# Second MLP of a three-block layer chain: other operand sums, relu placement, loads and residual adds on other engines

## The chip, the cores and the metric

The kernel runs on one core of one Trainium2 chip. The metric is the device time of one execution in microseconds; the figure of the kernel before is the median of three runs. A core has TensorE (PE, matmuls), VectorE (DVE), ScalarE (ACT), GpSimd (POOL) and SyncE (SP, which here only issues DMAs). The first four run their own instruction streams, each in order, and wait for each other by semaphores.

## The reference, cut to what matters

Three blocks follow each other on 8 sequences of 576 tokens and 512 channels: a linear attention, a gated MLP, and the block that the change is about:

```python
xt = x.transpose(0, 2, 1)
h = xt @ U @ V                          # token mixing of rank 32
u = x + h.transpose(0, 2, 1)
ch = np.maximum(u @ w_ch1, 0.0) @ w_ch2 # 512 -> 2048 -> 512
return (u + ch).astype(np.float32)
```

## The kernel before

All work up to `u` (attention, gated MLP, token mixing) takes the first 650 us; `u` is then in DRAM (`u2d`), transposed, channels on partitions, split into two token halves. What follows is `relu(u @ w_ch1) @ w_ch2`, in **5 groups** of columns: four of 480 and one of 384 tokens out of each half (`GROUPS`, L41).

**Seven products in place of eight.** Each of the two matrix products is done on 2 x 2 blocks with seven block products (indices 1 to 7, in the order 1, 2, 6, 7, 5, 4, 3, L42) by Winograd's form of Strassen's scheme. The operands of the products are sums and differences of the blocks of `u` (first product) or of relu'd `h` (second product): h11, h12, h21, h22. The weights' sums are made once, during the last sequences and the first group ("the conversion", `more`, L970: pieces that load, convert on VectorE, ScalarE and GpSimd, and store to the DRAM tiles `wd`).

**High and low operands.** For accuracy each fp32 operand is split into a high part of reduced precision (a ScalarE copy, `oh` or `uh`) and a low part, the rest (one VectorE operation, `ol` or `ul`); a product is high x high + low weight x high + high weight x low. So each step needs one ScalarE copy and then one VectorE "low" for its operand.

**Steps.** A group has 56 steps of 12 matmuls: 28 of the first product (for each of j = 0..3, a quarter of the middle layer, the seven indices), then 28 of the second (for each index, the four j). Below, r is the number of a step in its group, 0 to 55. In a step, `products` (L869) issues the matmuls and `after` (L935) what follows them. In the first product `after` drains PSUM on VectorE: partial sums `kept` and blocks `h`. In the second product the four j of an index accumulate in one PSUM buffer (four buffers exist), drained at j = 3; the finished block is added to the residual `u` (`store_res`, L916) and stored.

**Order.** In the loop over steps (L1256 on) VectorE, ScalarE, GpSimd and SyncE run in the order in which the program is written (`in_order`, L1003). In step s come: the weight fetch for step s + 4 on SyncE (`fetch`, five buffers `RING`; it waits for the matmuls of step s - 1), pieces of the conversion while there are any (two per step), the operand for step s + 3 (`h_prep`, L829; four buffers `OPS`), one of the sums in `later` (`h_diff`, L858), the matmuls, and `after`.

**Where things are made.** relu is taken again in each use: by ScalarE in the copy (L839), by VectorE in an operation that takes max(., 0) and adds or subtracts (`relu_minus`, L816); only h12 is relu'd in place by ScalarE (L946). For index 6, `h_prep` makes a temporary t and updates h21 besides the low (L848 to L856). The next group's blocks of `u` are loaded on GpSimd's queue (`u_load`, L745) and split and summed in half-width pieces during the second product (`u_prep`, L766; 22 VectorE operations). The residual is loaded on GpSimd's queue (L914), the kept sums are added to it by GpSimd (`with_kept`, L932), and GpSimd's queue stores the result (L926).

Of the kernel before, what the change touches and what calls it, by code (L numbers as in the profile page):

```python
# [22 lines left out]
def fused_kernel(tc, q, k, v, w_in, g_ln, w_sgT, b_sg, w_out, U, V, w_ch1, w_ch2, outT):  # L23
# [792 lines left out]
    def relu_minus(out, a, b, op=ALU.subtract):  # L816
        dve.scalar_tensor_tensor(out=out, in0=a, scalar=0.0, in1=b, op0=ALU.max, op1=op)  # L817

# [7 lines left out]
    def h_tile(j, slot, n):  # L826
        return ht[j, slot][:, :, 0:n]

    def h_prep(s):  # L829

        g, _, j, a = steps[s]
        n = GROUPS[g]
        hi, lo = (p2["ops"].tile([P, 2, NM], F32R, tag=x, name=x, bufs=OPS) for x in ("oh", "ol"))
        hs[s] = (hi, lo)
        hi, lo = hi[:, :, 0:n], lo[:, :, 0:n]
        h11, h12, h21, h22 = (h_tile(j, x, n) for x in (11, 12, 21, 22))
        if a in (1, 2, 3):
# [4 lines left out]
        if a == 5:  # L842
            act.activation(hi, h11, AF.Copy, scale=-1.0)
            dve.scalar_tensor_tensor(
                out=lo, in0=h11, scalar=-1.0, in1=as_f32(hi), op0=ALU.mult, op1=ALU.subtract
            )
            return
        if a == 6:  # L848
            t = p2["ops"].tile([P, 2, NM], F32, tag="t2", name="t2", bufs=1)[:, :, 0:n]
            relu_minus(t, h22, h11, ALU.add)  # L850
        else:
            t = {7: h12, 4: h21}[a]
        copy(hi, t)
        if a == 6:
            relu_minus(h21, h21, t)
        low(dve, lo, t, hi)  # L856

    def h_diff(g, j):  # L858

        n = GROUPS[g]  # L860
        h11, h12, h22 = (h_tile(j, x, n) for x in (11, 12, 22))
        relu_minus(h11, h11, h12)
        yield
        relu_minus(h12, h22, h12)
        yield
# [42 lines left out]

    def load_res(g, slot):
        n = GROUPS[g]  # L910
        mh, th = HALF[slot]
        t0 = starts[g]
        r = res[slot] = p2["res"].tile([P, 2, NM], F32, tag="res", name="res", bufs=2)[:, :, 0:n]
        pool.dma_start(r, u2d[th, 2 * mh : 2 * mh + 2, :, t0 : t0 + n].rearrange("c p t -> p c t"))  # L914

    def store_res(g, slot, bank):  # L916
        n = GROUPS[g]
        mh, th = HALF[slot]
        r = res.pop(slot)
        tt(dve, r, bank, r, ALU.add)  # L920
        t = starts[g]
        while t < starts[g] + n:
            b = t // HS
            e = min((b + 1) * HS, starts[g] + n)
            o = b * S + th * HS + t - b * HS
            pool.dma_start(  # L926
                outT[2 * mh : 2 * mh + 2, :, o : o + e - t].rearrange("c p t -> p c t"),
                r[:, :, t - starts[g] : e - starts[g]],
            )
            t = e  # L930

    def with_kept(slot, k):  # L932
        tt(pool, res[slot], res[slot], kept[k], ALU.add)

    def after(s):  # L935

        g, i, j, a = steps[s]
        n = GROUPS[g]
        bank = ps[a][:, :, 0:n]
        if i == 0:  # L940
            if a in PART:
                slot, k = PART[a]
                h = h_out(j, slot, n)
                tt(dve, h, bank, kept[k], ALU.add)
                if a == 3:
                    act.activation(h, h, AF.Relu)  # L946
            partial(a, n)
            return
        if j == 0 and a in (1, 2, 5, 4):
            load_res(g, {1: 11, 2: 22, 5: 21, 4: 12}[a])  # L950
        if j < NJ - 1:
            return
        if a in PART:
            store_res(g, PART[a][0], bank)
        partial(a, n)
        if a == 1:
            with_kept(11, 1)
        elif a == 7:
            with_kept(22, 7)
        elif a == 5:  # L960
            with_kept(21, 7)
        elif a == 4:
            with_kept(12, 1)
# [46 lines left out]
    OPS = 4  # L1010
# [237 lines left out]
    pool2("ust", 2, side="right")  # L1248
# [5 lines left out]
    later = deque()  # L1254
    ust_load = u_load(p2["ust"], 2)
    for s in range(len(ORDER), len(steps)):  # L1256
# [3 lines left out]
        if pieces or loaded or bounded or begun or merged or stores:  # L1260
            more(2)
# [5 lines left out]
        if ahead_s < len(steps) and steps[ahead_s][1] == 1 and r + OPS - 1 >= half_steps:  # L1267
            if r + OPS - 1 == half_steps:
                later.clear()
# [3 lines left out]
            if later:  # L1273
                if next(later[0], 0) == 0:
                    later.popleft()
                    if later:
                        next(later[0])
        products(s)
        after(s)
        if i == 1 and g + 1 < len(GROUPS):  # L1280
            if a == 7:
                if j == 0:
                    prep = u_prep(g + 1, (ust_load, ust_load))
                    next(prep)
            elif a in (5, 4, 3):
                for _ in range(2):
                    next(prep, None)
            if r == PER - 1:
                run(prep)
# [43 lines left out]
```

## Time and profile before

| | |
|---|---|
| median of the runs | 1401.33 us (1400.21 to 1406.36, 3 runs) |
| the profiled execution | 1399.94 us |
| its span, first to last instruction | 1398.1 us |
| mean granted TensorE clock | 0.986 of full speed; full from 650 us on |
| busy: PE, DVE, ACT, POOL | 1298.7, 1049.2, 605.0, 487.9 us |
| DMA traffic | 269 MB, mean 193 GB/s |

Busy times are sums over the whole span; the stages differ. A "window" row gives, for a stretch from A to B us, its length and then for each engine the busy time in it and the number of instructions that touch it. In lists of groups a row gives engine, operation, output<-inputs, shape, count, then busy us and mean ns of one, then the idle time before them and what ended it. In timelines a row gives start, duration, engine, line.

### The profile page before, as it was taken

What the parts mean: (1) busy time and instruction counts of PE and PEld (TensorE: products, weight loads), DVE (VectorE), ACT (ScalarE), POOL (GpSimd) and SP (SyncE); (2) the same over time, 40 slices, a digit from 0 to 9 for tenths busy, and PEclk for the clock granted to TensorE, in tenths of its full rate; (3) what the DMA queues carried; (4) which work ended last, traced back from release to release, by engine and by line L of the source; (5) the groups of instructions that cost most, each with busy time, mean ns of one, the idle gap of its engine ahead of it and who ended that gap; (6) DMA issues with size and microseconds to landing.
All of it is one profiled execution on the core that took longest, in us unless ns stands there. A gap on an engine that the chain in (4) does not pass through costs nothing.

```text
span 1398.1 us, 20610 instructions
## 1 busy us (share of the span) xinstructions
PE 1298.7 (93%) x7576; PEld 1150.5 (82%) x7576; DVE 1049.2 (75%) x1481; ACT 605.0 (43%) x969; POOL 487.9 (35%) x522
## 2 busy tenths in 40 slices
PE   4679999999999999967999999999999999999998
PEld 3578988889898988866887888878887888789987
DVE  7878868686868787686889864888469954986584
ACT  3764747474757565644333421243123411242132
POOL 5954455445444545574331210123003300131013
PEclk9889999999999999988999999999999999999999
DMA  7514243343433332348996876677667766688776
GB/s 241 166 33 145 61 153 112 103 132 102 125 109 111 121 107 99 135 159 278 343 361 224 294 241 205 211 260 257 210 202 256 255 229 204 201 277 283 248 241 206
DMA packets 116691, 269.16 MB, mean 193 GB/s; under 512 B 11888, under 2 KB 39824, under 8 KB 116592
## 3 DMA queue, kind: packets, MB, share of 16 engines
q1 hardware_dynamic: 109392, 240.53, 52.2%
q0 software_dynamic: 7200, 27.33, 5.8%
q8 instruction: 60, 0.98, 0.3%
q14 instruction: 39, 0.32, 0.1%
HBM read 219.58 MB, written 48.23 MB: 192 GB/s over the span
## 4 chain that ended last, share of the span: by engine, by line
PE 54%; DVE 23%; ACT 7%; issue 7%; POOL 5%; DMA 5%; SPq 0%; ACTq 0%; DVEq 0%; POOLq 0%
PE mm L49 37%; PE pv L49 6%; PE py L49 4%; DVE h L817 3%; DVE ol L52 2%; DVE ol L817 2%; PE px L49 2%; POOL qt L52 2%; DMA stg<-in_w_ch_dram 1%; DVE t L817 1%; DVE f L179 1%; DVE qt L52 1%; PE pp L49 1%; DVE gl L52 1%; DVE ul L52 1%
## 5 line engine op out<-in xcount | busy, mean ns | idle before, releaser
L49 PE MATMUL mm<-oh,wu 128*128 128x480 f32 (+1 forms) x1120 | 325.2, 371 | 5.4 <-ACT oh L58 5.4
L49 PE MATMUL mm<-uh,wu 128*128 128x480 f32 (+1 forms) x1064 | 308.4, 371 | 0.7 <-DVE h L52 0.7
L49 PEld LDWEIGHTS mm<-oh,wu 128*128 128x128 f32 x1120 | 207.4, 188 | 35.6 <-ACT oh L58 11.6
L49 PE MATMUL mm<-ol,wu 128*128 128x480 f32 (+1 forms) x560 | 211.0, 377 | 11.3 <-DVE ol L52 9.8
L49 PEld LDWEIGHTS mm<-uh,wu 128*128 128x128 f32 x1064 | 198.1, 188 | 27.2 <-DVE h L52 1.0
L49 PE MATMUL mm<-ul,wu 128*128 128x480 f32 (+1 forms) x532 | 198.1, 372 | 0.0
L52 POOL TENSOR_TENSOR res<-res,u 128x960 f32<-128x960 f32 (+1 forms) x20 | 58.6, 2928 | 377.0 <-ACT u L58 312.1
L52 DVE TENSOR_TENSOR h<-mm,u 128x960 f32<-128x960 f32 (+1 forms) x76 | 84.6, 1113 | 89.5 <-PE mm L49 89.4
L946 ACT ACTIVATE h<-h 128x960 f32<-128x960 f32 (+1 forms) x20 | 19.5, 974 | 265.2 <-DVE h L52 265.2
L49 PEld LDWEIGHTS mm<-ol,wu 128*128 128x128 f32 x560 | 105.0, 188 | 34.6 <-DVE ol L52 18.9
L52 POOL TENSOR_TENSOR chw<-f,chw 128x256 fp32r<-128x256 f32 x112 | 88.7, 807 | 99.2 <-ACT chw L58 93.5
L52 DVE TENSOR_TENSOR u<-mm,u 128x960 f32<-128x960 f32 (+1 forms) x72 | 80.0, 1111 | 48.7 <-PE mm L49 48.6
L49 PEld LDWEIGHTS mm<-ul,wu 128*128 128x128 f32 x532 | 99.9, 188 | 12.3
L926 POOL DMA_DIRECT2D out_dram<-res x44 | 31.9, 727 | 160.2 <-DVE res L52 160.2
L817 DVE SCALAR_TENSOR_TENSOR ol<-h,oh 128x960 fp32r<-128x960 f32 (+1 forms) x60 | 72.4, 1208 | 11.4 <-ACT oh L839 11.2
L58 ACT ACTIVATE chw<-f 128x256 fp32r<-128x256 f32 x112 | 43.3, 411 | 76.7 <-DVE f L180 23.4
L49 PE MATMUL py<-gh,wo_h 128*128 128x288 f32 x256 | 59.0, 313 | 14.4 <-ACT gh L58 5.2
L785 ACT ACTIVATE uh<-ust 128x480 fp32r<-128x480 f32 (+1 forms) x63 | 34.2, 578 | 70.4 <-DVE ust L52 70.4
L52 DVE TENSOR_TENSOR ul<-ust,uh 128x480 fp32r<-128x480 f32 (+1 forms) x54 | 58.3, 1111 | 7.8 <-ACT uh L785 7.8
L49 PE MATMUL py<-gl,wo_h 128*128 128x288 f32 x256 | 56.4, 303 | 8.3 <-DVE gl L52 8.1
L49 PE MATMUL pS<-sg_h,vh 128*128 128x288 f32 x256 | 55.8, 300 | 4.7 <-ACT ut L628 4.7
L52 POOL TENSOR_TENSOR vl<-ge,vh 128x512 fp32r<-128x512 f32 x32 | 46.0, 1439 | 35.8 <-ACT vh L58 35.7
(176 smaller groups left out, 2991.4 us busy)
## 6 DMA issues: line engine op xcount, KB each, us to landing
wu<-wd SPq DMA_DIRECT2D x280, 512.0 KB, 3.9
wd<-chw SPq DMA_DIRECT2D x112, 256.0 KB, 2.6
stg<-in_w_ch_dram SPq DMA_DIRECT2D x64, 256.0 KB, 3.0
u2d<-yt SPq DMA_DIRECT2D x32, 288.0 KB, 2.3
vt<-in_v_dram SPq DMA_DIRECT2D x32, 256.0 KB, 6.5
res<-u2d POOLq DMA_DIRECT2D x16, 480.0 KB, 5.0
qt<-in_q_dram SPq DMA_DIRECT2D x7, 1024.0 KB, 6.3
kt<-in_k_dram SPq DMA_DIRECT2D x7, 1024.0 KB, 6.1
```

Source lines behind the costliest of these rows:

```text
L49: pe.matmul(out, lhsT, rhs, start=first, stop=last)
L52: return eng.tensor_tensor(out=out, in0=a, in1=b, op=op)
L58: return act.activation(out, src, AF.Copy)
L179: dve.tensor_scalar(out=b, in0=b, scalar1=3, scalar2=None, op0=ALU.logical_shift_left)
L785: act.activation(hi, t, AF.Copy, scale=-1.0 if neg else 1.0)
L817: dve.scalar_tensor_tensor(out=out, in0=a, scalar=0.0, in1=b, op0=ALU.max, op1=op)
L926: pool.dma_start(outT[2 * mh : 2 * mh + 2, :, o : o + e - t].rearrange("c p t -> p c t"), r[:, :, t - starts[g] : e - starts[g]],)
L946: act.activation(h, h, AF.Relu)
```

## The change

The same products in the same order, with these differences:

- **Sums of h from other pairs, in place** (`h_sum`, `H_SUMS`): 7: h12 = h22 - h12; 6: h11 = h12 + h11; 4: h21 = h21 - h11; 5: h11 = h22 - h11. They stand at steps of their own: three sums 7 in the first product (r = 8, 15, 22), the rest at r = 28 + the key of `H_SUMS`. No temporary t.
- **relu on ScalarE, in place, for all four blocks** (`due`, `relu_due`), so a copy and a low are plain.
- **`OPS` five** instead of four: the operand for step s + 4 is prepared in step s.
- **The next group's `u`** in one tile of full width: loaded at r = 7 on SyncE's queue, summed in place by GpSimd at r = 12, 14, 16, 18 of the first product, copied and lowered at fixed steps of the second; three blocks are loaded again after their sums were used (for indices 1, 2, 3).
- **Residual**: loads and stores on SyncE's queue, stores issued one step later (`sent`, `send`); kept sums added by VectorE (`RES_KEPT`); slot 11 takes the index-1 product straight from PSUM. The last store of the kernel is made in two halves.
- **Conversion**: two pieces a step, three at every fourth step.

```diff
-        h11, h12, h21, h22 = (h_tile(j, x, n) for x in (11, 12, 21, 22))
-        if a in (1, 2, 3):
-            t = {1: h11, 2: h21, 3: h22}[a]
-            act.activation(hi, t, AF.Relu)
-            relu_minus(lo, t, as_f32(hi))
-            return
...
+        t = h_tile(j, {1: 11, 2: 21, 6: 11, 7: 12, 5: 11, 4: 21, 3: 22}[a], n)
+        copy(hi, t)
+        low(dve, lo, t, hi)
+
+    def h_sum(a, j, n):
+
+        h11, h12, h21, h22 = (h_tile(j, x, n) for x in (11, 12, 21, 22))
+        if a == 7:
+            tt(dve, h12, h22, h12, ALU.subtract)
+        elif a == 6:
+            tt(dve, h11, h12, h11, ALU.add)
+        elif a == 4:
+            tt(dve, h21, h21, h11, ALU.subtract)
+        else:
+            tt(dve, h11, h22, h11, ALU.subtract)
+
+    H_SUMS = {
+        -2: (6, 0), -1: (6, 1), 0: (6, 2), 1: (7, 3), 2: (6, 3), 4: (4, 0), 5: (4, 1), 6: (5, 0), 8: (4, 2),
+        9: (4, 3), 10: (5, 1), 12: (5, 2), 13: (5, 3),
+    }
...
+    U_AT = {6: (0, 0), 4: (1, 0), 5: (1, 1), 7: (0, 1), 1: (0, 0), 2: (1, 0), 3: (1, 1)}
+    U_LOW = {14: 6, 17: 4, 18: 5, 20: 7, 22: 1, 24: 2, 25: 3}
+    U_HIGH = {x - 2: a for x, a in U_LOW.items()}
+    U_SUMS = {12: 7, 14: 6, 16: 4, 18: 5}
...
+    def u_fetch(g, h, j):
+        n, t0 = GROUPS[g], starts[g]
+        sp.dma_start(u_at(h, j, n), u2d[j, 2 * h : 2 * h + 2, :, t0 : t0 + n].rearrange("c p n -> p c n"))
...
+        if r == 7:
+            us[0] = p2["ust"].tile([P, 2, 2, 2, NM], F32, tag="ust", name="ust")
+            for h in range(2):
+                for j in range(2):
+                    u_fetch(g, h, j)
+        elif r in U_SUMS:
+            u_sum(U_SUMS[r], n)
...
+    RES_LOAD = {-4: 11, 4: 22, 10: 21, 22: 12}
+    RES_KEPT = {16: (22, 7), 21: (21, 7), 26: (12, 1)}
...
+    def store_res(g, slot, bank, parts=1):
+        r = res.pop(slot)
+        for x in range(parts):
+            cs = slice(x * 2 // parts, (x + 1) * 2 // parts)
+            tt(dve, r[:, cs], bank[:, cs], r[:, cs], ALU.add)
+            sent.append(lambda cs=cs: put_res(g, slot, r, cs))
+
+    due = []
+
+    def relu_due():
+        while due:
+            h = due.pop()
+            act.activation(h, h, AF.Relu)
...
         if i == 0:
+            if a != 3:
+                relu_due()
             if a in PART:
                 slot, k = PART[a]
                 h = h_out(j, slot, n)
                 tt(dve, h, bank, kept[k], ALU.add)
+                due.append(h)
                 if a == 3:
-                    act.activation(h, h, AF.Relu)
+                    relu_due()
...
-    OPS = 4
+    OPS = 5
...
-            more(2)
+            more(2 + (s % 4 == 0))
...
             h_prep(ahead_s)
-            if steps[ahead_s][3] == 1:
-                later.append(h_diff(steps[ahead_s][0], steps[ahead_s][2]))
...
+        if r in (8, 15, 22):
+            h_sum(7, r // 7 - 1, GROUPS[g])
+        elif r - half_steps in H_SUMS:
+            h_sum(*H_SUMS[r - half_steps], GROUPS[g])
+        send()
+        if r - half_steps in RES_LOAD:
+            load_res(g, RES_LOAD[r - half_steps])
+        if r - half_steps in RES_KEPT:
+            slot, k = RES_KEPT[r - half_steps]
+            tt(dve, res[slot], res[slot], kept[k], ALU.add)
+        if g + 1 < len(GROUPS):
+            u_side(g + 1, r)
         products(s)
         after(s)
```

## Rows read from the trace of the kernel before

**Rows 1.** The page: busy us, share of the span and instructions of each engine

```profile
PE 1298.7 (93%) x7576; PEld 1150.5 (82%) x7576; DVE 1049.2 (75%) x1481; ACT 605.0 (43%) x969; POOL 487.9 (35%) x522
```

**Rows 2.** Windows: length, busy us (count) by engine, clock, DMA share, GB/s

```profile
679.41:734.55 55.14, 55.14 (x253) 47.41 (x254) 46.16 (x72) 21.35 (x46) 19.10 (x26) 1.00 1.00 364
734.55:813.41 78.86, 75.28 (x338) 62.16 (x336) 70.98 (x67) 32.10 (x39) 19.92 (x17) 1.00 0.74 254
813.41:886.77 73.36, 73.36 (x337) 63.07 (x336) 38.21 (x37) 10.58 (x12) 2.47 (x4) 1.00 0.65 219
886.77:965.60 78.83, 75.17 (x337) 62.19 (x336) 70.94 (x67) 32.09 (x39) 22.26 (x20) 1.00 0.72 245
...
1038.96:1117.52 78.56, 74.83 (x337) 62.32 (x336) 70.63 (x67) 32.11 (x39) 26.17 (x17) 1.00 0.72 247
...
1190.88:1268.63 77.75, 74.58 (x337) 62.35 (x336) 69.91 (x68) 31.23 (x39) 20.78 (x17) 1.00 0.73 245
...
1327.63:1391.41 63.78, 61.27 (x337) 58.20 (x336) 47.75 (x49) 21.93 (x27) 14.50 (x13) 1.00 0.73 241
923.01:948.95 25.94, 25.94 (x122) 22.52 (x120) 21.80 (x21) 11.55 (x14) 6.58 (x6) 1.00 0.79 282
1357.65:1378.65 21.00, 21.00 (x121) 21.00 (x121) 14.47 (x15) 8.46 (x10) 5.81 (x5) 1.00 0.79 254
```

**Rows 3.** Groups of VectorE's instructions in group 1's four index-6 steps, 908.2 to 923.01

```profile
L52 DVE TENSOR_TENSOR ol<-t,oh 128x960 fp32r<-128x960 f32 x4 | 4.6, 1158 | 0.0
L817 DVE SCALAR_TENSOR_TENSOR h<-h,t 128x960 f32<-128x960 f32 x3 | 3.5, 1158 | 0.1
L817 DVE SCALAR_TENSOR_TENSOR t<-h,h 128x960 f32<-128x960 f32 x3 | 3.5, 1154 | 0.1
```

**Rows 4.** Waits of TensorE, 734 to 1392 us: total us, times, longest

```profile
PE mm L49 <- DVE ol L52: 9.8, 20, 1.0
PE mm L49 <- ACT oh L58: 5.4, 9, 0.8
```

**Rows 5.** Timeline of GpSimd and VectorE around step 32 of group 1

```profile
898.40 3.25 POOL L52 TENSOR_TENSOR res<-res,u 128x960 f32<-128x960 f32 x1 [77.60 <-ACT u L58]
...
898.38 1.15 DVE L817 SCALAR_TENSOR_TENSOR h<-h,h 128x960 f32<-128x960 f32 x1
899.44 3.22 DVE L817 SCALAR_TENSOR_TENSOR ol<-h,oh 128x960 fp32r<-128x960 f32 x1
```

**Rows 6.** Timeline of GpSimd and VectorE in group 0's first half

```profile
725.07 1.45 POOL L52 TENSOR_TENSOR chw<-f,chw 128x256 fp32r<-128x256 f32 x2 [0.81 <-ACT chw L58]
...
724.79 1.15 DVE L52 TENSOR_TENSOR u<-mm,u 128x960 f32<-128x960 f32 x1
```

**Rows 7.** Timeline of VectorE and ScalarE at the head of group 1's second half

```profile
889.91 1.15 DVE L52 TENSOR_TENSOR h<-mm,u 128x960 f32<-128x960 f32 x1
893.03 1.16 DVE L817 SCALAR_TENSOR_TENSOR ol<-h,oh 128x960 fp32r<-128x960 f32 x1 [1.97 <-ACT oh L839]
...
891.09 1.00 ACT L946 ACTIVATE h<-h 128x960 f32<-128x960 f32 x1 [16.19 <-DVE h L52]
```

**Rows 8.** Groups of ScalarE's instructions by form, groups 1 to 3

```profile
L58 ACT ACTIVATE oh<-h 128x960 fp32r<-128x960 f32 x24 | 23.4, 999 | 9.4 <-PE mm L49 9.4
```

**Rows 9.** DMAs to landing: wu at 699:712; wu at 826:886; conversion at 679.41:734.55

```profile
DMA to landing us min/median/max: 5.1/6.7/7.3
...
wu<-wd SPq DMA_DIRECT2D x23, 512.0 KB, 3.3
...
wd<-chw SPq DMA_DIRECT2D x25, 256.0 KB, 5.6
stg<-in_w_ch_dram SPq DMA_DIRECT2D x8, 256.0 KB, 6.3
```

**Rows 10.** The chain that ended last, its end: start, us, what

```profile
1391.51 0.97 DVE res L52
...
1392.76 0.72 POOL out_dram L926
```

More of the change, by code (lines that the diff above doesn't have):

```diff
@@ L848, in h_prep @@
[L848 to L865, printed above, removed]
+        if a == 7:
[6 more added lines that the diff above has]
+            tt(dve, h11, h22, h11, ALU.subtract)
@@ new lines, in u_at, with u_sum @@
+    def u_at(h, j, n):
+        return us[0][:, :, h, j, 0:n]
+    def u_fetch(g, h, j):
+        n, t0 = GROUPS[g], starts[g]
+        sp.dma_start(u_at(h, j, n), u2d[j, 2 * h : 2 * h + 2, :, t0 : t0 + n].rearrange("c p n -> p c n"))
+    def u_sum(a, n):
+        u11, u12, u21, u22 = (u_at(h, j, n) for h in range(2) for j in range(2))
+        if a == 7:
+            tt(pool, u12, u22, u12, ALU.subtract)
+        elif a == 6:
+            tt(pool, u11, u12, u11, ALU.add)
+        elif a == 4:
+            tt(pool, u21, u21, u11, ALU.subtract)
+        else:
+            tt(pool, u22, u22, u11, ALU.subtract)
@@ new lines, in u_side @@
+    def u_side(g, r):
+        n = GROUPS[g]
+        if r == 7:
[5 more added lines that the diff above has]
+            u_sum(U_SUMS[r], n)
+        r -= half_steps
+        if r in U_HIGH:
+            a = U_HIGH[r]
+            uc[g, a] = tuple(
+                p2["uc"].tile([P, 2, NM], F32R, tag=f"{x}{a}", name=f"{x}{a}") for x in ("uh", "ul")
+            )
+            copy(uc[g, a][0][:, :, 0:n], u_at(*U_AT[a], n))
+        if r in U_LOW:
+            a = U_LOW[r]
+            hi, lo = (x[:, :, 0:n] for x in uc[g, a])
+            low(dve, lo, u_at(*U_AT[a], n), hi)
+            if a in (6, 4, 5):
+                sent.append(lambda: u_fetch(g, *U_AT[a]))
@@ L925, in store_res @@
             o = b * S + th * HS + t - b * HS
[L926 to L928 removed]
+            sp.dma_start(
+                outT[2 * mh + cs.start : 2 * mh + cs.stop, :, o : o + e - t].rearrange("c p t -> p c t"),
+                r[:, cs, t - starts[g] : e - starts[g]],
             )
             t = e
[L932 to L933 removed]
+    def store_res(g, slot, bank, parts=1):
[9 more added lines that the diff above has]
+            act.activation(h, h, AF.Relu)
     def after(s):
@@ L944, in after @@
                 tt(dve, h, bank, kept[k], ALU.add)
+                due.append(h)
                 if a == 3:
-                    act.activation(h, h, AF.Relu)
+                    relu_due()
             partial(a, n)
             return
-        if j == 0 and a in (1, 2, 5, 4):
-            load_res(g, {1: 11, 2: 22, 5: 21, 4: 12}[a])
         if j < NJ - 1:
             return
+        if a == 1:
+            tt(dve, res[11], bank, res[11], ALU.add)
         if a in PART:
[L954 to L963, printed above, removed]
+            end = a == ORDER[-1] and g == len(GROUPS) - 1
+            store_res(g, PART[a][0], bank, 2 if end else 1)
+        if a != 3:
+            partial(a, n)
     pieces = deque()
@@ L1267, in fused_kernel @@
         if ahead_s < len(steps) and steps[ahead_s][1] == 1 and r + OPS - 1 >= half_steps:
-            if r + OPS - 1 == half_steps:
-                later.clear()
             h_prep(ahead_s)
-            if steps[ahead_s][3] == 1:
-                later.append(h_diff(steps[ahead_s][0], steps[ahead_s][2]))
[L1273 to L1277, printed above, removed]
+        if r in (8, 15, 22):
[10 more added lines that the diff above has]
+            u_side(g + 1, r)
         products(s)
         after(s)
[L1280 to L1289, printed above, removed]
+    send()
     part.__exit__(None, None, None)
```

22 lines of the change are left out of this document (8 added, 14 removed).

## The prediction, made before the changed kernel was run

> **What bounds the kernel now.** I read the page first [rows 1]: TensorE is busy 93% of the span, so only what idles it can be won. Then the windows by half [rows 2]. A step is 12 matmuls. In ten steps without a stall it takes 25.94 / 10 = 2.594 us (480 columns) or 21.00 / 10 = 2.100 us (384 columns, the last group). 28 such steps make 72.6 and 58.8 us. The first products need 73.36 us each with TensorE busy throughout: nothing is to be had there. The second products take 78.86, 78.83, 78.56, 77.75 and 63.78 us, which is 6.2 + 6.2 + 5.9 + 5.1 + 5.0 = 28.4 us over. (The busy column hides half of that, since a waiting matmul is drawn longer; the step count is the safer measure.) The waits of TensorE over this stretch [rows 4] name the low halves (ol) of the operands, made by VectorE, and the high halves (oh), made by ScalarE. The groups of VectorE in the four steps of index 6 [rows 3] show why: each step needs t, the update of h21 and ol, 1.154 + 1.158 + 1.158 = 3.47 us, on one engine in a step of 2.59. VectorE, with 70.9 of 78.83 us busy in this half [rows 2], is the limit there and has no reserve.
>
> One more row counts against the second half: at its step 32 GpSimd's residual sum started at 898.40, and the VectorE operation beside it took 3.22 instead of 1.15 us [rows 5], a loss of 2.07 us just ahead of the index-6 steps. A VectorE operation that reads PSUM keeps its 1.15 us beside GpSimd [rows 6].
>
> **Part 1, block sums of the middle layer and relu.** Before, each of the 4 j costs VectorE 7 lows and 4 sums; after, the same 11, so nothing is saved in number or kind (all 1.15 us, 1.07 from start to start when queued [rows 5]). What changes is when. Sum 7 of three j goes into the first product (steps 8, 15, 22), where VectorE is 38.2 of 73.36 us busy; two sums 6 go to steps 26 and 27; the other 11 stand one to a step. I count per step of the second half (x = step - 28) lows, sums, residual adds, drains and lows of the next tokens: never over two, but for x = 19 with three. Two queued operations are 2.14 us of 2.59, so VectorE gains 0.45 us on TensorE in each step. In all: 24 lows, 11 sums, 8 drains, 3 residual adds and 7 token lows = 53 x 1.07 = 57 us, where it now has 70.9. Relu moves to ScalarE: 3 more a j at 1.00 us [rows 7], 12 us a first product in which ScalarE has 10.58 of 73.36 busy: covered.
>
> **Part 2, operands five deep.** The copy for step s + 4 is issued at step s, one step earlier. It waits for TensorE to leave step s - 1, done by then. It gives each low four steps (10.4 us) from issue to use.
>
> **Part 3, the head of each second half,** the only place where the queue is still deep. Steps 24 to 27 hold 4 lows, 2 sums and 5 drains, 11 x 1.07 = 11.8 us in 10.5. Before, the last drain there ended 4.3 us into the half (889.91 + 1.15 - 886.77), ScalarE's relu waited for it, then the copies, and VectorE idled 1.97 us until 893.03 [rows 7]. After, two relus (h12, then h21) stand ahead of the copy: drain ends at +3.5 to +4.3, relus 2.0, copy 1.0 [rows 8], so the first low starts at +6.5 to +7.3 and ends by +8.5. It is due four steps in, at +10.4: 1.9 us to spare, growing by 0.45 a step. Value taken: no stall. Bounds: 0 to 2.5 us a group if the drains slip.
>
> **Part 4, token sums on GpSimd, loads on SyncE.** Lows of the next tokens are 7 x 1.15 at full width instead of 22 half-width ones, and the four sums leave VectorE. The last steps of the half, which held 22 such pieces, then have two VectorE operations or fewer. The sums (steps 12, 14, 16, 18) run beside drains that read PSUM, which are not slowed [rows 6]. The Trainium skill (SBUF — State Buffer, "Who interferes with whom") says that GpSimd and a VectorE instruction with two SBUF inputs block each other for the whole instruction: that speaks against sums on GpSimd wherever VectorE works on SBUF. Rows 5 agree (2.07 us). By that rule groups 1 to 3 lose at most one such block on sum 7 at step 15, in a half with 35 us of spare VectorE time: still nothing.
>
> Loads and stores move from GpSimd's queue to SyncE's, which also fetches the weights. In a quiet first product a fetch lands in 3.3 us [rows 9], of four steps (10.5): 7 us of slack. Four token blocks of 480 KB (1.97 MB) ahead of it at step 7 take, at group 0's 364 GB/s [rows 2], 5.4 us: covered in groups 1 to 3. A store waits on SyncE for VectorE's add, 3 to 5 us into the step by part 3, and holds the next fetch 1 to 2 us: covered by the same 7.
>
> **Part 5, group 0's first half is not covered.** There the DMA engines are busy all the time at 364 GB/s [rows 2], a fetch takes 6.7, at most 7.3 us to land [rows 9], so 10.5 - 7.3 = 3.2 us are left. The token blocks (before: on GpSimd's queue in the second half) now come at step 7 of this half: 5.4 us, and the queue has no hole to take them. The conversion of the weights runs at 2.25 pieces a step instead of 2; its 33 transfers (25 + 8, [rows 9]) of 256 KB are 0.72 us each, so 12 steps on, 3 more have gone out ahead: 2.2 us. Without any spare rate TensorE waits 5.4 + 2.2 - 3.2 = 4.4 us. If the engines can go faster than their mean, down to 0. A second cost sits on VectorE: 46.16 of 55.14 us busy, 9.0 idle; three sums (3.2) and four GpSimd sums that each block it up to 2.07 (8.3) make 11.5, 2.5 us too much, which the four PSUM buffers take (TensorE may be three steps ahead, 7.8 us) unless it reaches part 3's 1.9 us: 0 to 2 us. Bounds 0 to 6.4; I take 3.0, nearer to the full queue than to the empty one, since a stall also gives the queue time. The Trainium skill (DMA: Bandwidth & Descriptors, "Specifications") gives about 358 GB/s as one core's HBM limit; by that there is no spare rate and the term would be 4.4, the total 1375. The row's 364 is at that limit.
>
> **Part 6, the end.** The last add takes 0.97 us, then GpSimd issues two stores, 0.72 each (the first is shown, [rows 10]). After, the add is in two halves, with SyncE's issues: at best 0.48 + 1.44 = 1.9 us less, at worst 0; I take 1.0.
>
> **Sum.** The profiled run took 1399.94 (span 1398.1 and 1.8 around it), 1.4 below the median of the runs. 1399.9 - 28.4 + 3.0 - 1.0 = 1373.5, say 1373.
>
> **Rivals.**
> - *The head of the halves binds (part 3).* For: ScalarE is in order, two relus precede the copy, 1.9 us spare. Against: that spare is measured from a drain as late as today's. Price: 2.5 us x 5, and 4.4 for part 5 instead of 3.0: 1387.
> - *The stall only moves.* The new waits (fetches behind the token batch in every first half, the head of the half) give back what the sums won: 4 x 5.4 = 22 us if the fetch slack in groups 1 to 3 were used up by other traffic, with 2.5 x 2 at heads: about 1397, no change. Against: 7 us of slack for 5.4.
> - *Slower: one in-order SyncE queue.* Each of the 20 stores waits there for VectorE's add with weight fetches behind it. It decides once VectorE runs more than 7 us behind TensorE at a store; at 10 us behind, 3 us are lost at each: 20 x 3 = 60, less the 28 won: about 1430. For: once the conversion is over, that queue now holds only fetches, which wait for TensorE alone. Against: 53 operations fill 57 of 72.6 us, and an operation would have to take over 1.35 us for VectorE to fall behind at all.
> - *It does not do what it says:* VectorE's count is unchanged, so if the index-6 steps were bound by ScalarE's copies (5.4 us of the waits [rows 4]) part of the stall stays: 1373 + 5 = 1378, inside the range.
>
> **How the numbers follow.** Forecast with its bounds (1368 to 1379, the fourth rival in it) 0.72; head of the halves 0.14; stall moves 0.07; slower 0.07. Low end: part 5 at 0 and part 6 at 1.9 give 1369.6, and 2 us below for what the heads may win besides. High end: the first rival less little, 1385. Half a per cent, 7 us, is about what a measurement of this kernel tells from no change. Faster 0.86, same 0.07, slower 0.07.
>
> **What would show it.** Second products of 72.6 us (58.8 in the last group) with VectorE near 57 us; first products still 73.4; no wait for ol in the index-6 steps; GpSimd idle in second halves; fetch landings of 10 us or more and a few us of TensorE idle in steps 12 to 24 of group 0. I am wrong if the second halves stay above 75 us, if TensorE waits for wu after step 40, or if steps 32 to 35 wait for ol.

## The result and the profile after

The changed kernel took **1385.73 us** in the median (1384.32 to 1386.15, 4 runs) beside 1401.31 us (1400.21 to 1406.36, 4 runs) for the kernel before: a ratio of 0.988, with a 95% interval of 0.9855 to 0.9905. It is faster, by 15.6 us. The forecast was 1373, and the range's upper end, 1385, lies 0.7 us below the median, so the time came out just beyond the range. The sum promised 26.4 us and 15.6 came.

The profiled execution took 1385.37 us. Its page shows the change of engines that the prediction described [rows 1]: VectorE and GpSimd lose work, ScalarE gains some. In the chain that ended last TensorE has 62% (54% before).

```profile
PE 1293.8 (94%) x7576; PEld 1156.3 (84%) x7576; DVE 1015.3 (73%) x1442; ACT 656.3 (47%) x1001; POOL 407.3 (29%) x438
...
PE 62%; DVE 14%; ACT 6%; DMA 6%; issue 6%; POOL 5%; SPq 1%; DVEq 0%; ACTq 0%; POOLq 0%
```

The windows of the same halves answer to [rows 2]: length, busy us and count of PE, PEld, DVE, ACT, POOL, then granted clock, DMA share, GB/s. The rows are group 0's first half from its step 7, its second half, both halves of group 1, and the second half of the last group.

```profile
679.39:748.38 68.99, 59.82 (x253) 49.25 (x253) 52.68 (x73) 29.00 (x55) 29.34 (x29) 0.95 0.92 326
748.38:822.61 74.23, 73.29 (x337) 62.81 (x336) 63.03 (x59) 33.66 (x36) 0.00 (x0) 1.00 0.78 267
822.61:895.98 73.37, 73.37 (x338) 63.06 (x336) 39.31 (x35) 20.89 (x22) 9.04 (x4) 1.00 0.70 242
895.98:968.59 72.61, 72.61 (x338) 63.04 (x337) 59.92 (x56) 32.42 (x34) 0.00 (x0) 1.00 0.79 262
...
1322.54:1381.50 58.96, 55.95 (x320) 55.63 (x318) 41.27 (x48) 21.83 (x27) 0.00 (x0) 1.00 0.74 251
```

Three of the five rows are what was forecast: second halves of 72.61 and 58.96 us with no stall, VectorE at 56.70 to 59.92 us in the longer ones, GpSimd at 0.00, first halves unchanged at 73.37. Group 0's second half is 1.6 us over. The waits of TensorE from 748.38 to 1382 us (total, times, longest) say the same. Where [rows 4] had 15 us of waits for operands, all that is left is

```profile
PE mm L49 <- DMA wu<-wd: 0.6, 1, 0.6
PE mm L49 <- DVE ol L52: 0.3, 1, 0.3
```

The first row is the one that is far off: the 21 steps that took 55.14 us [rows 2] take 68.99. Set against the trace of before, from step to step:

| stretch | before | after | difference | forecast |
|---|---|---|---|---|
| up to step 0 | 649.82 | 650.07 | +0.2 | 0 |
| group 0, first half (28 steps) | 84.73 | 98.31 | **+13.6** | +3.0 |
| group 0, second half | 78.86 | 74.23 | -4.6 | -6.2 |
| groups 1 to 4, to the last step | 575.75 | 553.62 | -22.1 | -22.2 |
| last step and end of the program | 8.96 | 7.29 | -1.7 | -1.0 |
| sum | | | -14.6 | -26.4 |

The missing 11.8 us are 10.6 in one half of one group and 1.6 in the next half; the other rows give back 0.4.

### The profile page after: what moved, and what is told of

Same layout as the page of the kernel before. It is cut to its first block, busy times and chain, and to the rows that moved or that the text cites. A ratio compares the mean times of both kernels' runs of the same rounds, so it can differ in the third digit from the quotient of the medians.

```text
span 1383.5 us, 20618 instructions
## 1 busy us (share of the span) xinstructions
PE 1293.8 (94%) x7576; PEld 1156.3 (84%) x7576; DVE 1015.3 (73%) x1442; ACT 656.3 (47%) x1001; POOL 407.3 (29%) x438
## 4 chain that ended last, share of the span: by engine, by line
PE 62%; DVE 14%; ACT 6%; DMA 6%; issue 6%; POOL 5%; SPq 1%; DVEq 0%; ACTq 0%; POOLq 0%
PE mm L49 46%; PE pv L49 6%; PE py L49 4%; DMA wu<-wd 2%; PE px L49 2%; DMA stg<-in_w_ch_dram 1%; POOL chw L52 1%; DVE f L179 1%; DVE qt L52 1%; DVE f L180 1%; POOL qt L52 1%; PE pt L682 1%; DVE gl L52 1%; POOL gt L52 1%; PE pp L49 1%
## 5 line engine op out<-in xcount | busy, mean ns | idle before, releaser
L49 PEld LDWEIGHTS mm<-oh,wu 128*128 128x128 f32 x1120 | 208.7, 188 | 26.4 <-issue 1.0
L49 PE MATMUL mm<-ol,wu 128*128 128x480 f32 (+1 forms) x560 | 208.2, 372 | 0.3 <-DVE ol L52 0.3
L986 ACT ACTIVATE h<-h 128x960 f32<-128x960 f32 (+1 forms) x80 | 75.7, 970 | 225.8 <-DVE h L52 225.8
L52 DVE TENSOR_TENSOR ol<-h,oh 128x960 fp32r<-128x960 f32 (+1 forms) x140 | 155.8, 1113 | 34.1 <-ACT oh L58 30.3
L58 ACT ACTIVATE oh<-h 128x960 fp32r<-128x960 f32 (+1 forms) x140 | 131.5, 969 | 96.7 <-PE mm L49 81.0
L52 POOL TENSOR_TENSOR ust<-ust 128x960 f32<-128x960 f32 (+1 forms) x16 | 34.7, 2180 | 385.2 <-DMA ust<-u2d 247.5
L52 DVE TENSOR_TENSOR h<-h,h 128x960 f32<-128x960 f32 (+1 forms) x80 | 89.1, 1114 | 12.4 <-ACT h L986 12.4
L58 ACT ACTIVATE u<-mm 128x960 f32<-128x960 f32 (+1 forms) x24 | 22.2, 926 | 84.2 <-PE mm L49 55.3
L49 PE MATMUL pu<-xh,wih 128*128 128x288 f32 x256 | 57.3, 306 | 1.4 <-ACT ut L628 0.7
```

The source lines that it names most:

```text
L49: pe.matmul(out, lhsT, rhs, start=first, stop=last)
L52: return eng.tensor_tensor(out=out, in0=a, in1=b, op=op)
L58: return act.activation(out, src, AF.Copy)
```

## Where group 0's first half lost its time

The waits of this stretch (679.39 to 748.38), of TensorE first, then of ScalarE and VectorE, name a chain and not one culprit. (In the kernel before, TensorE has a single wait here, of 0.7 us.)

```profile
PE mm L49 <- DVE h L52: 3.8, 3, 2.7
PE mm L49 <- DMA wu<-wd: 2.6, 2, 1.6
PE mm L49 <- issue: 2.5, 1, 2.5
PE mm L49 <- DVE u L52: 1.0, 1, 1.0
...
ACT chw L58 <- DMA wd<-chw: 10.7, 2, 6.3
...
DVE f L179 <- ACT f L173: 5.0, 1, 5.0
```

The weights are still being converted here. ScalarE writes each converted piece into a buffer (chw), which must first have been stored (wd<-chw). ScalarE waited 10.7 us for these stores. The exponent (line 173) stands behind that in ScalarE's order, VectorE waited 5.0 us for the exponent, and its drains (h, u) are what TensorE waited for. The fetches (wu) are 2.6 us of it. This is read from the waits alone; the experiments below show that ScalarE and VectorE can wait as long without any cost. The DMAs of 683 to 698.2 us show what the stores shared the DMA engines with: the four token blocks (ust) came from step 7 on, and everything near them lands in 6.4 to 7.5 us (issues, KB, median us to landing; [rows 9] has 5.6 for the stores and 6.3 for the loads over the half).

```profile
wu<-wd SPq DMA_DIRECT2D x5, 512.0 KB, 7.0
ust<-u2d SPq DMA_DIRECT2D x4, 480.0 KB, 6.4
wd<-chw SPq DMA_DIRECT2D x6, 256.0 KB, 6.9
stg<-in_w_ch_dram SPq DMA_DIRECT2D x4, 256.0 KB, 7.5
```

Then come GpSimd's token sums. The timeline shows VectorE's short operations beside them, and the same operations alone (start, us):

```profile
705.22 4.89 POOL L52 TENSOR_TENSOR ust<-ust 128x960 f32<-128x960 f32 x2
720.19 2.27 POOL L52 TENSOR_TENSOR ust<-ust 128x960 f32<-128x960 f32 x1
...
708.05 2.35 DVE L180 SCALAR_TENSOR_TENSOR f<-stg,f 128x256 uint32<-128x256 uint32 x1
710.64 0.43 DVE L180 SCALAR_TENSOR_TENSOR f<-stg,f 128x256 uint32<-128x256 uint32 x1
720.49 2.11 DVE L167 TENSOR_SCALAR stg<-stg 128x256 f32<-128x256 f32 x1
723.41 0.28 DVE L167 TENSOR_SCALAR stg<-stg 128x256 f32<-128x256 f32 x1
```

An operation of 0.43 us takes 2.35 and one of 0.28 takes 2.11: each ends 0.2 to 0.3 us after GpSimd's sum, as if it had gone on only then. In [rows 5] the VectorE operation, of 1.15 us when alone, ends 1.0 us after the sum. Last, the granted clock in windows of 1 us:

```profile
712.00:713.00 1.00, 0.81 (x4) 0.72 (x5) 0.76 (x3) 0.83 (x1) 0.00 (x0) 1.00 1.09 287
714.00:715.00 1.00, 1.00 (x4) 0.83 (x3) 0.00 (x0) 1.00 (x3) 0.55 (x1) 0.50 0.84 344
...
732.00:733.00 1.00, 1.00 (x4) 0.79 (x4) 0.77 (x2) 1.00 (x2) 0.68 (x1) 0.50 0.00 0
```

TensorE had stood idle for 2.65 us before 712.19, and for 2.49 us before 730.85 (the "issue" of the list, for which the profile shows no releaser; VectorE's drain `u` ended at 730.75). Near each the clock fell to 0.50 (1.2 GHz) for about 3.4 us, and a pair of matmuls took 1.00 instead of 0.60 us. At a mean clock of 0.95 over 68.99 us this is 3.4 us. The kernel with doubled loads, at the end of the experiments, runs the same program up to the end of this half. Its stretch took 69.28 us at a mean clock of 0.98: there the clock stayed at 1.00 after a wait of 2.65 us, and fell once, at a later one of 2.50. The row at 732 also has a DMA share of 0.00: the "full" queue moved nothing there. SyncE issued no DMA between 725.85 and 732.71, since the store at its head waited for a piece that GpSimd had yet to convert (SyncE's waits from 690 us to the end of the half):

```profile
SPq L355 <- POOL chw L52: 22.1, 12, 6.4
```

That wait alone costs little: over the 21 steps it is 23.7 us here, 12.8 before, and 22.0 in a kernel below whose 21 steps lose 1.5 us.

This names the chain, not what each part of the change puts into it. For that the experiments take them apart.

## Experiments

Their halves of group 0 and their total are read as above. The stretch up to step 0, which no edit touches, took 649.7 to 653.1 us from one profiled execution to another, so stages are compared by their own length and totals by the medians. Steps 0 to 6 of group 0 scatter too: 28.4 to 30.1 us in the kernels without extra conversion pieces there, mostly by one wait for a drain (h) before step 2, 0.8 to 3.5 us. So what the loads, the sums and the conversion cost is read from steps 7 to 27, the 21 steps of the windows, and not from the whole half. Two of the kernels (loads and sums late, and only the sums late) compute one operand of group 1 (index 5 of its first product) from a block that had been loaded again, and wait for that load, so what they return is not the reference's; this touches no length in group 0's first half, but it does touch the second half and the total.

**Part 1 alone.** The kernel before with block sums and relu of the change, four operands deep, tokens and loads as they were:

```diff
-        if a in (1, 2, 3):
-            t = {1: h11, 2: h21, 3: h22}[a]
-            act.activation(hi, t, AF.Relu)
...
+        t = h_tile(j, {1: 11, 2: 21, 6: 11, 7: 12, 5: 11, 4: 21, 3: 22}[a], n)
+        copy(hi, t)
+        low(dve, lo, t, hi)
```

> The kernel before with one part of the change alone: the sums of h from other pairs in place and relu on ScalarE in place; four operands deep, token blocks, residual and stores as before. Theory (this part carries the gain in the second halves, the losses come from the loads): second halves of groups 1 to 3 at 72.6 to 74 us, the last at 58.9 to 60, group 0's first half at 84 to 87: 1371 to 1377. Rival C (three more relus a quarter hold up ScalarE's queue in group 0): first half above 90 us. Rival D (the fifth operand and VectorE freed of the half-width pieces are needed too): second halves stay above 75 us, 1385 or more.

Measured: 1380.46 us (1378.97 to 1380.96), ratio 0.9843 (0.9827 to 0.9859). **That is 5 us faster than the whole change.** Group 0's first half from step 7, and group 1's second half:

```profile
680.98:736.11 55.13, 55.13 (x253) 47.41 (x253) 43.84 (x72) 28.27 (x54) 20.03 (x26) 1.00 0.97 355
886.61:960.58 73.97, 73.42 (x338) 62.80 (x337) 67.30 (x64) 33.32 (x40) 21.38 (x20) 1.00 0.78 262
```

So the relus on ScalarE cost nothing (28 us busy of 55, no stall), and the sums at steps of their own give 4.9 of the 6.2 us of a second half. The other parts together give the last 1.4 in group 1 (73.97 to 72.61); no run takes them apart. The total is 3.5 us beyond the range expected. Most of that stands at the head of group 0's second half (77.16 us): the last drain ended 6.9 us into the half and the first low at +10.9, past the +10.4 of part 3, and steps 30 and 31 lost 2.9 us. There the head did bind.

**The residual sums alone.** The kernel before with one line changed:

```diff
-        tt(pool, res[slot], res[slot], kept[k], ALU.add)
+        tt(dve, res[slot], res[slot], kept[k], ALU.add)
```

> The kernel before; only the four sums of kept parts into the residual move from GpSimd to VectorE, in their old places. Theory (the index-6 steps are bound by three VectorE operations of 1.16 us; GpSimd's sum at step 32 made one VectorE operation 2.07 us longer and costs what TensorE loses at steps 34 and 35): the index-6 steps stay at 3.5 us, steps 34 and 35 fall from 2.65 and 3.14 to 2.6, a second half of groups 1 to 3 from 78 to 79 to 77 to 78. Rival (the port lock is the main cause of the stall): second halves fall to 75 us or less.

Measured: 1397.3 us (one execution). Group 1's second half is 78.04 us:

```profile
888.00:966.04 78.04, 74.52 (x337) 62.42 (x336) 68.11 (x72) 32.19 (x39) 10.86 (x15) 1.00 0.74 247
```

The steps ahead of index 6 are back at 2.59 us, but the four index-6 steps still take 14.5 us instead of 10.4. The block by GpSimd [rows 5] was worth 0.8 us here and 1.8 in group 2; the three VectorE operations of each index-6 step [rows 3] are untouched by this edit, and the steps stay near their 3.5 us. In group 0 the half came out longer, 79.83 us for 78.86.

**Group 0's loads and sums late.** Loads at step 24 instead of 7, sums on VectorE in the second half:

```diff
-        if r == 7:
+        if r == (24 if g == 1 else 7):
...
-        elif r in U_SUMS:
+        elif g == 1 and r in U_SUMS_0:      # 31, 35, 39, 43
+            u_sum(U_SUMS_0[r], n, dve)
+        elif g > 1 and r in U_SUMS:
```

> The changed kernel, but while group 0 runs, the next group's blocks of u are loaded at step 24 instead of 7 and summed by VectorE at steps 31, 35, 39 and 43 instead of by GpSimd at 12 to 18; groups 1 to 3 as changed. Theory (the four loads at step 7 of group 0 hold up the conversion's stores and loads in SyncE's queue, ScalarE and VectorE wait for these in order, and TensorE for VectorE): group 0's first half falls from 98.3 to 85 to 88 us, its second half stays within 73 to 77, in all 1372 to 1376 us. Rival A (the quicker conversion, 2.25 pieces a step, is the cause): first half stays above 95 us, 1383 or more. Rival B (GpSimd's sums block VectorE): as the theory here; the next run tells them apart.

**Only the sums late**, the loads stay at step 7 (the second half of that diff):

> As the run before, but the loads stay at step 7; only the sums of group 0 move to VectorE's steps 31 to 43. Theory (loads): group 0's first half keeps most of its loss, 93 to 98 us, 1380 to 1385 in all. Rival B (GpSimd's sums, which in this trace made four VectorE operations 1.0 to 1.9 us longer each): the first half falls to 86 to 89 us, 1373 to 1377. If both take a share, it lies between, and the share is read from the half.

Measured: 1379.35 (1378.41 to 1379.78), ratio 0.9836 (0.982 to 0.9851), and 1383.0 (1381.87 to 1385.34), ratio 0.9865 (0.9847 to 0.9883). Steps 7 to 27, loads late and loads at 7:

```profile
680.80:738.09 57.29, 56.08 (x253) 47.10 (x254) 46.17 (x73) 29.05 (x55) 20.16 (x25) 1.00 0.96 347
```

```profile
681.59:744.63 63.04, 56.49 (x252) 46.92 (x253) 46.89 (x73) 29.21 (x55) 20.36 (x25) 1.00 0.98 352
```

The loads at step 7, with no sum beside them, cost 63.04 - 57.29 = 5.8 us more than loads at 24. With both late the first half is 86.78 us, as expected; but the loads at 24 still meet a full queue and cost 5.5 us at steps 28 and 29 (a wait of 3.8 us for a fetch, and 3.4 us at half clock behind it), so the second half, 78.23, and the total are beyond what was expected. With only the sums late the half is 92.43, between the two figures: both take a share.

What TensorE waited for with the loads at step 7 and no sums beside them is not VectorE (steps 7 to 27):

```profile
PE mm L49 <- DMA wu<-wd: 6.2, 5, 2.0
PE mm L49 <- DVE h L52: 1.1, 2, 0.7
```

In the same steps ScalarE waited 14.9 us for the stores and VectorE 5.3 us for the exponent, more than in the change. In the part-1 kernel these waits are 7.8 and 4.9 us, and TensorE lost nothing. So the loads reach TensorE through late weight fetches, the way that the prediction had named, and the chain through ScalarE and VectorE is not what makes them cost.

**Which queue, which engine.** First the sums at their steps 12 to 18, but on VectorE; then the loads at step 7, but on GpSimd's queue (sums late):

```diff
-            u_sum(U_SUMS[r], n)
+            u_sum(U_SUMS[r], n, dve if g == 1 else pool)
```

> The changed kernel, but group 0's four token sums at steps 12, 14, 16 and 18 run on VectorE instead of GpSimd; its loads stay at step 7 and the conversion at 2.25 pieces a step. If GpSimd's sums cost by blocking VectorE (about 2 us each, four times), group 0's first half falls from 98.3 to 92 or below, the time to about 1379. If the loads in SyncE's queue at step 7 carry the loss and the sums only add to an engine that is waiting anyway, the half stays at 96 or above, the time at 1383 to 1386.

```diff
-        sp.dma_start(u_at(h, j, n), u2d[...])
+        (pool if g == 1 else sp).dma_start(u_at(h, j, n), u2d[...])
```

> The changed kernel with group 0's token loads still at step 7, but issued on GpSimd's queue as in the kernel before, and its token sums on VectorE at steps 36, 38, 40, 42. If the loss is the traffic (1.97 MB more in a half whose engines are full), group 0's first half stays at about 92.4, as with the loads at step 7 on SyncE's queue and the sums late. If it is the order in SyncE's queue (the loads stand ahead of the weight fetches and hold them), the half falls to about 86, the time to 1377.

Measured: 1380.68 (1378.54 to 1383.83), ratio 0.9859 (0.9845 to 0.9874), and 1378.91 (1377.95 to 1380.13), ratio 0.9845 (0.9832 to 0.9859).

```profile
682.38:746.84 64.46, 57.25 (x252) 46.56 (x253) 50.04 (x77) 28.94 (x55) 21.10 (x25) 1.00 0.94 342
```

```profile
680.29:742.47 62.18, 57.88 (x253) 48.12 (x253) 45.25 (x72) 28.64 (x54) 23.96 (x29) 0.97 0.97 355
```

The 21 steps take 64.46 us with VectorE's sums against 68.99 with GpSimd's: putting them on GpSimd costs 4.5 us. The whole half, 93.76, lies between the two expected figures: neither "92 or below" nor "96 or above". The clock stays at 1.00 here, so up to 3.4 of the 4.5 are the two falls of the clock. The sums also take GpSimd's own time (29.34 us busy against 21.10), with pieces of the conversion behind them in its order; no run tells that from the blocking of VectorE. With the loads on the other queue the half is 92.26, beside 92.43 on SyncE's, and the 21 steps are 62.18 beside 63.04. **It is mostly the traffic, not the order in SyncE's queue.** The clock fell once in the kernel with the other queue, for 3.4 us after a wait of 2.68; without the 1.7 us that this cost its 21 steps would be 60.5, so the order can make up to 2.5 us. The Trainium skill (DMA: Bandwidth & Descriptors, "Issuing engines are not separate DMA queues") says that DMAs run on the same 16 engines whichever engine starts them; the near-equal stretches agree. (The median is still 4 us lower: this kernel's second half takes 73.85 us against 78.00, where the other's sums stand at other steps and one of them waits for a load.)

**The conversion back at two pieces a step,** loads and sums as in the change (the conversion then ends later, and the first preparation of h moves one step back):

```diff
-            more(2 + (s % 4 == 0))
+            more(2)
```

> The changed kernel with two conversion pieces at every step of the loop (no third one at each fourth step); group 0 begins to prepare operands at step 25 instead of 24, with two in that step. Theory (loads): the pace matters little, at most 2 us: 1382 to 1386. Rival A (pace): group 0's first half falls below 90 us, 1377 or less.

Measured: 1382.72 (1380.54 to 1383.18), ratio 0.9862 (0.9844 to 0.988). The two halves of group 0:

```profile
678.09:738.68 60.59, 57.14 (x252) 46.58 (x253) 45.30 (x69) 28.80 (x54) 28.44 (x29) 1.00 0.96 341
738.68:817.84 79.16, 75.19 (x338) 63.91 (x338) 66.75 (x62) 34.18 (x37) 0.00 (x0) 0.98 0.79 269
```

The first half falls by 9.4 us to 88.96 (the 21 steps by 8.4, with 3.4 of it the clock), and the second gives 4.9 back, since its operands start late: steps 28, 31 and 32 take 4.7, 4.7 and 4.9 us, and TensorE waited there for oh and ol. The total is in the range of the theory, but the half fell below 90 us, as rival A had it, and not by the 2 us at most that the theory allowed. So the costs are not additive: taken back from the whole change the faster conversion is worth 8.4 us of the 21 steps, and added to the kernel without loads and sums there it costs 1.5, as the next kernel shows. Whether it is needed once loads and sums are out of its way, no run shows.

**Loads after the conversion.** Group 0's blocks are loaded at steps 32 to 34, when nothing is converted any more, and summed by VectorE at 36, 38, 40 and 42. The second kernel also takes the conversion's five extra pieces out of the queue's busiest stretch: at steps 0, 2, 4, 6, 8 instead of 8, 12, 16, 20, 24. The third has them at 3, 4, 5, 6, 8.

```diff
+    U_SUMS_0 = {36: 7, 38: 6, 40: 4, 42: 5}
+    U_LOAD_0 = {32: ((1, 1), (0, 1)), 33: ((0, 0),), 34: ((1, 0),)}
...
-                more(2)                          # steps 0 to 6
+                more(2 + (s % 2 == 0))           # third kernel: s >= 3
...
-            more(2 + (s % 4 == 0))
+            more(2 + (s == 8))
```

> The changed kernel; only while group 0 runs, the next group's blocks of u are loaded after the conversion (steps 32, 33, 34) instead of at step 7, and summed by VectorE at steps 36, 38, 40 and 42. Theory (group 0's first half has no reserve on the DMA engines and little on VectorE; work put there costs TensorE time, the same work after the conversion does not): first half 85 to 88 us (the conversion's pace costs 2, as with the loads at step 24), second half 73 to 76 instead of the 78.2 with loads at step 24, the others unchanged: 1374 to 1377 us. Rival (VectorE has no room for four more sums in group 0's second half, or the loads meet a backlog there too): second half 78 us or more, 1379 or more.

> As the run before, and the conversion's extra pieces stand at steps 0, 2, 4, 6 and 8 instead of 8, 12, 16, 20 and 24. Theory: in steps 0 to 6 TensorE waits for other work anyway, so the extras cost little there and the two us of the pace come back: first half of group 0 (from step 0) 84 to 86.5 us, 1372 to 1376 in all. Rival (the extras lengthen the start, where VectorE is busy too): steps 0 to 6 take 32 us instead of 29.5, and nothing is won over the run before.

> The same kernel as b3_loads_late_extra_early, in more rounds: 1372 to 1375 if its 1373.2 holds, 1376 if it is no better than the kernel with the loads after the conversion alone (1376.1).

> As b3, but the conversion's five extra pieces at steps 3 to 6 and 8, away from steps 1 and 2, in which the kernel b3 lost 3.6 us to VectorE. If that loss is the extra pieces' work on VectorE there, group 0's first half falls from 88.9 to about 86, the time to 1370 or 1371; if the rate of the transfers sets it, it stays at 1373.

Measured, with the halves of group 0 in the profiled execution:

| kernel | median us | ratio, 95% | first half | second half |
|---|---|---|---|---|
| the change | 1385.73 | 0.988 (0.9855 to 0.9905) | 98.31 | 74.23 |
| loads after the conversion | 1376.09 | 0.9828 (0.9808 to 0.9847) | 85.02 | 75.51 |
| and extra pieces at 0, 2, 4, 6, 8 | 1373.23 | 0.9804 (0.9786 to 0.9822) | 88.92 | 73.04 |
| the same again | 1371.87 | 0.9796 (0.9782 to 0.9809) | 87.34 | 73.36 |
| extra pieces at 3, 4, 5, 6, 8 | 1372.37 | 0.9794 (0.9781 to 0.9808) | 84.54 | 72.97 |

The first of these has the change's conversion rate and a first half of 85.02, 0.3 from before's 84.73. But its steps 0 to 6 happened to be 1.2 us shorter; the 21 steps, the first row below, take 56.61 against 55.14: **the rate alone costs 1.5 us.** The last one's steps 7 to 27, the second row, take the kernel before's time to the hundredth [rows 2], without one stall in TensorE behind step 7; the third row is its second half:

```profile
678.61:735.22 56.61, 55.86 (x252) 47.10 (x253) 46.00 (x73) 28.91 (x55) 20.24 (x25) 1.00 0.98 350
682.30:737.43 55.13, 55.13 (x253) 47.41 (x253) 45.02 (x72) 29.68 (x53) 16.64 (x22) 1.00 1.00 363
737.43:810.40 72.97, 72.91 (x338) 62.89 (x337) 65.42 (x62) 31.84 (x34) 0.00 (x0) 1.00 0.80 284
```

Loads after the conversion came out as expected in both halves and in the total. With extra pieces at 0, 2, 4, 6 and 8 steps 0 to 6 took 33.35 and 31.21 us, as the rival had it (32), and the half stayed above the 84 to 86.5 expected; with the pieces from step 3 on they took 29.41 and the half fell by 2.8 to 4.4 us. Whether VectorE's work on the pieces is the cause isn't shown: the wait for a drain before step 2 was 3.58 and 2.28 us in the two profiles and 1.17 with the pieces from step 3 on, but it is 0.8 to 3.5 us in kernels without extra pieces there. The medians of the last three don't differ by more than their runs do, and that they lie 2.9 to 4.2 us below the kernel with late loads alone is hardly clear either: that kernel's runs reach from 1373.46 to 1379.15, and its fastest is the profiled one. All of them are 24 to 28 us below the kernel before.

**One queue in order: its price.** In groups 1 to 3 every token block is loaded twice into the same tile:

```diff
                 for j in range(2):
                     u_fetch(g, h, j)
+                    if g > 1:
+                        u_fetch(g, h, j)
```

> The changed kernel with each of the four token blocks loaded twice at step 7 of groups 1 and 2 (for groups 2 and 3) and 3; nothing else. It tells what the fetch's reserve is in a quiet first half. Theory (one queue in order; 1.97 MB took 4.3 us of the reserve of 7.0, leaving 2.7): the second load takes another 4.5 to 5.4 us, so TensorE waits 1.8 to 2.7 us for wu around steps 11 to 13 in each of the three groups, their first halves 75.2 to 76.1 instead of 73.37. Rival (queues share, later fetches overtake or the rate rises under load): first halves stay at 73.4.

Measured: 1427.4 us (one execution), and not by the cause that was meant. The second load of a tile waits in SyncE's queue until the first has landed. SyncE's waits (835 to 880 us), then TensorE's in the same first half:

```profile
SPq L871 <- DMA ust<-u2d: 17.8, 4, 5.3
...
PE mm L49 <- DMA wu<-wd: 13.8, 1, 13.8
```

So it says nothing of added traffic, and leaves the fetches' reserve in a quiet half untested. It shows what a held queue costs: 17.8 us of waiting in front of the weight fetches make group 1's first half 88.96 us, 15.6 longer. Of these 13.8 are the stall, and 1.7 the step behind it at half clock.

## Why the prediction was right, and where it failed

**Parts 1 and 2 were right,** to 0.1 us a group: second halves of 72.61 and 58.96 us against 72.6 and 58.8, and VectorE's count of 57 us against 56.70 to 59.92. That an index-6 step asks 3.47 us of VectorE was the cause: the part-1 kernel takes these operations apart and the steps fall to 2.59 us, and the residual-sum kernel leaves them and the steps stay at 3.5. The fifth operand of part 2 was not tried by itself.

**Part 3 was right, with more to spare.** The head of group 1's second half (step 28 starts at 895.98):

```profile
898.41 1.15 DVE L52 TENSOR_TENSOR h<-mm,u 128x960 f32<-128x960 f32 x1
902.42 1.16 DVE L52 TENSOR_TENSOR ol<-h,oh 128x960 fp32r<-128x960 f32 x1 [2.86 <-ACT oh L58]
...
899.60 1.90 ACT L986 ACTIVATE h<-h 128x960 f32<-128x960 f32 x2 [5.57 <-DVE h L52]
901.40 3.68 ACT L58 ACTIVATE oh<-h 128x960 fp32r<-128x960 f32 x4
```

The drain ends at +3.6, two relus take 1.9, the copy follows, and the first low ends at +7.6 where +8.5 was allowed and +10.4 is the limit: 2.8 us to spare, not 1.9. In the changed kernel the rival in which the head binds is refuted; in group 0 of the part-1 kernel, four operands deep, it did bind.

**Part 4 was right for groups 1 to 3:** first halves of 73.37, no stall. (The VectorE operations beside GpSimd's four sums read PSUM there and kept 1.15 to 1.16 us.) The slack of the fetches behind the token batch fell from 7 us to 2.7 at the least, and behind a residual store that waited for VectorE's add to 2.0 us (SyncE's waits, 895.98 to 968.59):

```profile
SPq L968 <- DVE res L52: 6.1, 3, 4.4
```

The third rival's mechanism is there, at the 3 to 5 us forecast, with 2.0 us left before it costs anything. With the queue held longer it does cost, as the doubled loads show.

**Part 5 failed: the term of 3.0 us, bounds 0 to 6.4, measured 13.6.** Both halves of its working were too small. Taken in this order, the 21 steps are 55.14 us before, 56.61 with the faster conversion, 63.04 with the loads at step 7, 64.46 with VectorE's sums at steps 12 to 18, and 68.99 with these on GpSimd; steps 0 to 6 were 0.3 us shorter. In another order the shares differ, as the conversion at two pieces a step shows.

- *The traffic.* It said 5.4 + 2.2 us of transfers less a reserve of 3.2: at most 4.4. Measured: conversion rate and loads at step 7, with no sums beside them, make the 21 steps **7.0 us (loads on GpSimd's queue) to 7.9 us (SyncE's) longer**, 1.5 of it the rate. The path was right, since TensorE waited for the fetches; the sizes were not. The landings of the fetches in the traces give them. Call the time by which a fetch lands ahead of its use its lead. Counted from the start of step 7, the weights of step 27 landed 2.7 us later than before with part 1 alone, which costs no time but uses lead, 6.5 us later with the faster conversion, and 12.5 us later with the loads as well. So the step that failed is the term of 2.2 us for what comes ahead of the fetches besides the loads: it measured 6.5. The loads' 5.4 measured 6.0. The reserve of 3.2 was there, and larger: the lead of step 27 fell from 5.2 us to 0.6, and the other 7.9 us TensorE waited.
- *Why 2.2 became 6.5* is not shown. The prediction counted bytes alone; but the fetches also stand in SyncE's order behind stores that wait for GpSimd's pieces, and that wait is 12.8 us over the 21 steps before, 18.7 with part 1 and 22.0 with the faster conversion. No run takes it away by itself. In the change itself the bytes are 326 GB/s x 68.99 us = 22.5 MB where before had 364 x 55.14 = 20.1, and the difference at 364 GB/s is 6.7 us of the 13.9. Nor is 364 a limit: in the kernel with the loads at step 24 the engines moved 405 GB/s from 728 to 745 us. The prediction took from the Trainium skill (DMA: Bandwidth & Descriptors, "Specifications") about 358 GB/s as one core's HBM limit; this measurement goes beyond it.
- *VectorE.* It said 2.5 us too much work, at most 2.0 on the path, since four PSUM buffers let TensorE run ahead. Measured: 1.4 us for the sums' place (64.46 against 63.04 with them late) and 4.5 for putting them on GpSimd, 5.9 in all. The size of a block was right (2.35 for 0.43, 2.11 for 0.28); the cover wasn't there. With sums in the half TensorE's waits pass from the fetches to VectorE's drains (4.9 of 7.8 us with VectorE's sums, against 1.1 of 7.3 with the sums late). In the change it stopped for 2.65 and 2.49 us, and the clock took up to 3.4 on top, a cost that the prediction hadn't on its list. How much of the 4.5 is the blocking, how much GpSimd's own time and how much the clock stays open.

The Trainium skill's rule of shared SBUF access (SBUF — State Buffer, "Who interferes with whom"), by which GpSimd and a VectorE instruction with two SBUF inputs block each other for the whole instruction, was weighed and set aside for groups 1 to 3, rightly (their first halves stay at 73.37); in group 0 the trace agrees with it (2.35 us for 0.43). What it cost there lies within the 4.5 us.

**Part 6** measured 1.7 us for a forecast of 1.0 (bounds 0 to 1.9). **Group 0's second half** kept 1.6 us of stall: 0.6 at step 32, 0.2 at 36, and 0.9 at 40 and 41, where a fetch is still late.

**The rivals.** "The stall only moves" was the nearest in kind: nearly half of the gain was given back, in one place (group 0) and not in every half as its price assumed. "Doesn't do what it says" is refuted. That the time lies within 1 us of the range's upper end is luck: that end stood for heads that bind in five groups, and they cost nothing. The rest of the sum held: with group 0's loads moved behind the conversion and its extra pieces moved early the total comes to 1372, 1.5 above the sum without its part 5 (1370.5).

## What to carry to other kernels

A prefetch that is free in four stages of five can cost most of a change in the fifth: place it by stage, and where the DMA engines are full, count what it does to the readers' lead, and not its bytes alone: here three parts of one change drew on the same lead, and what went beyond it was time. Read the cost of a part from the steps that it touches, since others scatter by more than it may cost. When a change has several parts, time the one that carries the gain alone; here it beat the whole by 5 us, and the rest paid only once group 0's loads had moved.

## What was not expected of the hardware

- Near the end of waits of 1.90 to 2.68 us of TensorE, in stretches with stalls, or just behind them, the granted clock went to 0.50 for 3.4 us in four kernels, so that such a stall cost about 1.7 more. It is no rule: the same program, profiled again, kept its clock at 1.00 after a wait of 2.65 us.
- A short VectorE operation beside a GpSimd sum lasts until just behind that sum's end, however short it is: 0.28 us became 2.11. The price goes by GpSimd's operation, not by VectorE's.
- A second load into a tile waits in its queue for the first one's landing (5.3 us at the longest), with everything issued behind it.
